# LSH attention and gated MLP on one core: one GpSimd addition for two heads, dearer planned residual loads, wide zero products, first low words on GpSimd

## The chip, the cores and the metric

One Trainium2 chip, one of its cores. The metric is the time of one execution on the device in microseconds (us); the median of several executions is compared. Engines: PE is TensorE, DVE is VectorE, ACT is ScalarE, POOL is GpSimd, SP is SyncE, which issues nearly all the DMAs here.

## The reference, cut to what matters

Batch 4, 8 heads, 768 positions, head size 64; then a gated MLP of width 512 with 1024 hidden columns.

```python
q_bits = (einsum(q, proj) > 0); k_bits = (einsum(k, proj) > 0)      # 6 bits, a bucket each
scores = where(q_bucket == k_bucket, q @ k.T / 8, -1e9)
attn = exp(scores - max); attn = attn / (sum(attn) + 1e-9)
x = concat_heads(attn @ v)
h = gelu(x @ w_in); u, v = split(h)
v_s = w_sg @ (layer_norm(v) * g_ln) + b_sg
out = x + (u * v_s) @ w_out
```

## The kernel before, in words

Every tensor that goes through PE in one pass is split into a high part (rounded by ACT) and a low part (the rest), and products are made of high and low parts. Work is done on pairs of heads: 16 pairs, the 128 partitions holding two heads of 64.

**For each pair** `load` brings q and k (the raw tile of each has one buffer, so the next pair's load waits until the last reader of the raw tile is done), `parts` transposes them on PE (line 543, six products each), copies them back by ACT (553), and makes the high part on ACT (547) and the low part on DVE (550). The first pair's bit features come from two products per tensor with `pwd` (586) and comparisons on DVE (589); the later pairs' features (570, 573) are scattered by DMA. `largest` makes the scores of one tile of 128 queries and takes the row maxima on DVE (616, 621); it runs `AHEAD` = 4 tiles ahead. `weigh` makes transposed scores of a key tile (656), the exponentials for both heads on ACT (661), and adds them up over the key tiles on POOL (674): before, one addition of 384 columns for each head, 5 additions per head and half, 320 in all, 64 of which are the first of a sum and read two tiles p. `weighted` makes p times v (686) and `total` the sums over partitions (710); `finish` sends sums through DRAM, takes reciprocals (729) and writes x transposed to DRAM (735).

**Between the pairs** twelve weight jobs (395 to 405: seven operations on DVE, one on POOL and one on ACT each) decode the MLP weights. **The MLP** follows batch by batch: `load_x` (835 to 840), `hidden_v` (882), `hidden_u` (913), `gate` (931), `project` (960). In the first batch, `gate_weights` also loads the transposed gate weights (851), transposes them on DVE (852), and splits them on ACT (853) and POOL (854), tile by tile, in a ring with eight buffers, so that a later tile's load waits until an earlier tile's transposition has begun. `project` adds the residual: `rx` is loaded from DRAM with 512 runs of 128 bytes per DMA (953), four DMAs for each tile of 128 positions, and transposed by DVE (956). It has two buffers.

**The order.** No engine's order is written by hand. Every operation is given to `Plan.add` with an engine, a planned cost, and a priority (smaller goes first). `Plan.order` simulates the engines with these costs and takes for each engine the ready operation with the smallest priority; the resulting order is then fixed in the program. In the real run every engine and every DMA queue goes through its list in that order and waits at the head of it. A planned cost is thus no time on the chip; it decides what stands behind what. Operations marked `port` (the POOL ones, and DVE ones with two SBUF operands) are planned so that POOL and DVE exclude each other. The numbers at the top of the file are offsets to priorities: `HID` to `hidden_v` of the first batch, `MLP` to its weights and loads, `SHAPE` and the `O.` lists to single operations.

**The lead** (lines 453 to 458) has zero products on PE before the first q arrives: five and four products of 128 columns of zeros, with six small transpositions between them in the source, which in the trace run after all nine.

```python
nc.tensor.matmul(psb[:, 6, :P], msts[0][:, 0].bitcast(F32), msts[0][:, 0].bitcast(F32), start=True, stop=True)   # 453, 458
dma(p0 - 30, 0.4, lambda eng, rx=rx, g=g, t=t: eng.dma_start(...), xd[b], [(rx, g)])                             # 953
```

Of the kernel before, what the change touches and what calls it, by code (L numbers as in the profile page):

```python
# [9 lines left out]
F32 = mybir.dt.float32  # L10
# [8 lines left out]
DRAM = bass.MemoryType.DRAM  # L19


MLP = {"xl": "POOL", "gm": "DVE", "gl": "POOL", "wg": 457.72, "wo": -69.99, "x": 480}

NSUM = 3
BANKED = False
HID = 267.73
AVP = 3.07
S0P = -1.32
AHEAD = 4
PREP, SHIFTP, FINP, WSTEP, WP = 10.27, -7.36, 10, 9.69, 23.41  # L30
LOADS = "SP"
GPLACE = 4
XLATE = 5.18
FIRST = -5
FEAT = 3.92
LOWP = 8.16
LOADP = 1.16
LATF = 3.2
OM = [0.01, 0.27, 0.0, 2.44, 0.37, 0.0, -1.25, 0.68, 0.49, 1.13, -0.06, 0.0]
OW = [0.0, 0.2, 0.0, 0.29, 0.0, 0.0, 0.0, 0.0, -0.69, 0.48, 0.0, 1.07]  # L40
# [3 lines left out]
OL = [-0.28, -0.4]  # L44
OH = [2.49, 0.0]
OT = [1.05, 0.73]
OF = [1.53, -2.21]
RATE = 2.73
WFROM = 1.42
ADDW = 1  # L50


SHAPE = {"A": [-0.81, -2.62, -0.81, -0.81, -0.81, -0.12, -0.81, -2.53, -0.81, -0.81, -0.81, -0.81, -0.81, -0.81, -0.81, -0.81, -0.81, -3.5, -0.81, -0.81], "AV": [0.04, 0.0], "C": [4.55, 2.17, 2.17, 4.28], "E": [0.0, 0.0, -1.65, -0.24, 1.16, 0.0, 0.0, 0.0, 0.36, 0.0, -2.01, 0.0], "M": [0.0, 0.0, 0.0, 0.0, 0.0, 0.0, 0.0, 0.0, 0.0, -0.91, 0.0, 0.0], "R": [0.0, 0.0, 0.0, 0.0, 0.0, 0.0, 0.0, -0.16, 0.0, -1.68, 0.0, 0.0], "S": [3.78, 0.75], "T": [0.0, 0.1], "W": [0.0, 0.0, 0.0, 0.0, 0.0, 0.0, 0.0, 0.0, 0.0, 0.0, 0.0, 0.0], "hi": [3.88, -3.27], "lo": [0.0, 0.0], "m": [1.89, -3.45], "rc": [-2.26, 0.77], "sm": [3.72, -0.88], "un": [1.1, 4.96], "xt": [3.13, -0.6], "F": [-0.28], "sg": [-0.66], "x": [0.35, 0.35]}


class Plan:
# [218 lines left out]
def kernel(  # L275
# [16 lines left out]
    nc = tc.nc  # L292

    B, H, S, D = q.shape
    P = 128
    NT = S // P
    HT = NT // 2
    SH = S // 2
# [10 lines left out]
    Q = 32  # L309
# [22 lines left out]
    msts = [const.tile([P, HT, P], F32R, name=f"m{i}") for i in range(2)]  # L332
# [78 lines left out]
    PE, DVE, ACT, POOL, SP = "PE", "DVE", "ACT", "POOL", "SP"  # L411
    xs = [dram.tile([DM, S], F32, name=f"xs_{b}") for b in range(B)]

    plan = Plan()
# [5 lines left out]
    xd = [[plan.buf(f"xd_{b}_{c}", 1) for c in range(NC)] for b in range(B)]  # L420
# [28 lines left out]

    ps_s = Pool("ps_s", "left", PSUM)  # L450
    psb = ps_s.pool.tile([P, 8, 512], F32, name="psb", tag="psb", bufs=1)
    for i in range(5):
        nc.tensor.matmul(psb[:, 6, :P], msts[0][:, 0].bitcast(F32), msts[0][:, 0].bitcast(F32), start=True, stop=True)
    for i in range(6):
        nc.tensor.transpose(psb[:, 7, i:i + 1], frow[:, i, :], ident[:1, :1])
    nc.vector.tensor_copy(fcol, psb[:, 7, 0:6])
    for i in range(4):
        nc.tensor.matmul(psb[:, 6, :P], msts[0][:, 0].bitcast(F32), msts[0][:, 0].bitcast(F32), start=True, stop=True)
    for s in range(2):
        for j in range(2):  # L460
            for r in range(2):
# [12 lines left out]
    if True:  # L474
# [61 lines left out]
        def parts(st, s, prio):  # L536

            hh, lo, raw, fac, tp = st.hi[s], st.lo[s], st.raw[s], (SCALE, 1.0)[s], ps_two()

            def tr():  # L540
                for hf in range(2):
                    for i in range(HT):
                        nc.tensor.transpose(tp()[:, hf, i * P:(i + 1) * P],
                                            raw()[:, hf * HT + i].rearrange("p j d -> p (j d)"), ident)

            def high():
                nc.scalar.mul(hh(), x_of(raw), fac)

            def low():
                nc.vector.scalar_tensor_tensor(lo(), x_of(raw), fac, hh().bitcast(F32), op0=ALU.mult, op1=ALU.subtract)  # L550

            plan.add(PE, 0.654, prio, tr, [raw], [tp], tag="T")
            plan.add(ACT, 0.81, prio, lambda: nc.scalar.copy(x_of(raw).rearrange("p (a b) -> p a b", a=2), tp()[:, :, :SH]), [tp], [raw], tag="x")
            def split(p1, p2):
                plan.add(ACT, 0.81, p1 + OH[s], high, [raw], [hh], tag="hi")
                plan.add(DVE, 0.98, p2 + OL[s], low, [raw, hh], [lo], port=True, tag="lo")

            st.split.append(split)

        def x_of(raw):  # L560
            return raw().rearrange("p t j d -> p (t j d)")
# [193 lines left out]
        def rest(st, prio):  # L755
# [32 lines left out]
        for n in range(NPAIR):  # L788
            for c in range(NT):
                if c == 0 and n + 2 < NPAIR:  # L790
                    prepare(n + 2, 2 * (g_ := NT * n) + PREP)
                hf, k0, g = c // HT, 2 * (c % HT), NT * n + c
# [9 lines left out]
                if c == 1 and GPLACE <= n < GPLACE + NT:  # L802
                    t = n - GPLACE
# [11 lines left out]

    M_ = MLP
    b1, b2 = Pool("b1", "right"), Pool("b2", "right")
# [5 lines left out]

    g_bc = b2.ring([P, FH], F32, "g_bc")

    def dma(prio, us, fn, r=(), w=(), e=SP):
        eng = nc.sync if e == SP else nc.scalar
        plan.add(e, 0.55, prio, lambda: fn(eng), r, w, dma=us)

    def load_x(b, prio):  # L830
        r = []
# [115 lines left out]
    def project(b, gs, prio):  # L947
        ov = out[b].rearrange("(t p) m -> p t m", t=NT)
        for t in range(NT):
            ts_, hf, p0 = slice(t * P, (t + 1) * P), t // HT, prio + t  # L950
            rx, po, ob = tile_of([P, DM], F32, "rx", 2), ps_one(), tile_of([P, DM], F32, "ob", 2)
            for g in range(P // Q):
                dma(p0 - 30, 0.4, lambda eng, rx=rx, g=g, t=t: eng.dma_start(
                    rx()[g * Q:(g + 1) * Q].rearrange("b (f a) -> b f a", a=Q),
                    xs[b][:, t * P + g * Q:t * P + (g + 1) * Q].rearrange("(f b) a -> b f a", b=Q)), xd[b], [(rx, g)])
            plan.add(DVE, 0.7, p0 - 5, lambda rx=rx, ob=ob: nc.vector.transpose(ob(), rx()), [rx], [ob])
            for f, (gh, gl) in enumerate(gs):
                def mm(f=f, gh=gh, gl=gl, po=po, ts_=ts_):
                    for n, (a, w) in enumerate(((gh, woh), (gh, wol), (gl, woh))):
                        nc.tensor.matmul(po(), a()[:, ts_], w()[:, f, :], start=(f == 0 and n == 0), stop=(f == NF - 1 and n == 2))  # L960
                plan.add(PE, 0.685, p0 + 0.01 * f, mm, [(gh, hf), (gl, hf), (woh, f), (wol, f)], [po])

            plan.add(DVE, 0.7, p0, lambda ob=ob, po=po: nc.vector.tensor_add(ob(), po(), ob()), [po, ob], [ob])  # L963
            dma(p0, 0.73, lambda eng, ob=ob, t=t: eng.dma_start(ov[:, t, :], ob()), [ob])


    xx = load_x(0, HID - 20)
# [55 lines left out]
```

## Time and profile before

| | |
|---|---|
| median of three executions | 734.95 us (734.49 to 736.82) |
| the profiled execution | 734.26 us, of it 732.5 us from the first to the last instruction |
| PE busy | 719.4 us, 98% of the span |
| DVE, POOL, ACT busy | 529.2, 471.7, 381.0 us |
| mean granted clock of PE | 0.998 |

The busy times are shares of the whole span; the stages differ, and PE's busy time includes the modelled end of each product. The table of stages among the rows below shows where PE is not busy. A row of the timeline gives the start, how long a run of equal instructions lasts, the engine, the line, and in brackets the idle time before it with what ended it.

### The profile page before, as it was taken

The numbers are of one execution on the slowest core, as the hardware profiler recorded it, in microseconds if no ns is written. First come the engines' busy times: TensorE is split into PE (matmuls) and PEld (weight loads), VectorE is DVE, ScalarE is ACT, GpSimd is POOL, SyncE is SP. The second block draws the span as 40 slices with busy tenths as digits, with TensorE's granted clock in tenths as the row PEclk, the third lists the DMA queues.
The fourth block names the chain that finished last, engine by engine and source line by source line (L and its number), as shares of the span: only waits on it lengthen the run. The fifth ranks groups of instructions, "written<-read, shape, count | busy, mean of one in ns | idle before, by whom it ended". The sixth has DMA issues, their size and how long they took to land. (4 is left out here: it accounts for less than half of the span.)

```text
span 732.5 us, 14275 instructions
## 1 busy us (share of the span) xinstructions
PE 719.4 (98%) x5304; PEld 570.6 (78%) x5304; DVE 529.2 (72%) x783; ACT 381.0 (52%) x611; POOL 471.7 (64%) x452
## 2 busy tenths in 40 slices
PE   8999999999999999999999999999999999999997
PEld 6777676766767676776767669888999889988996
DVE  6888779997899998788899258455863586348733
ACT  2666576666657656665756547421761066106510
POOL 2589799998898987897898957551553045404230
PEclk9999999999999999999999999999999999999999
DMA  6314643644665455255532135814221601061004
GB/s 129 85 44 103 132 130 94 136 106 124 166 143 133 103 117 139 68 133 137 136 101 65 59 110 138 193 48 127 47 65 37 146 14 44 0 148 26 0 1 116
DMA packets 177766, 70.39 MB, mean 96 GB/s; under 512 B 157728, under 2 KB 167968, under 8 KB 177696
## 3 DMA queue, kind: packets, MB, share of 16 engines
q1 hardware_dynamic: 176464, 68.62, 39.1%
q8 instruction: 42, 0.69, 0.5%
q10 hardware_dynamic: 1232, 0.86, 0.4%
q14 instruction: 28, 0.23, 0.1%
HBM read 51.61 MB, written 17.24 MB: 94 GB/s over the span
## 5 line engine op out<-in xcount | busy, mean ns | idle before, releaser
L674 POOL TENSOR_TENSOR sum<-sum,p 128x384 f32<-128x384 f32 x256 | 247.1, 991 | 44.5 <-ACT p L661 39.5
L621 DVE TENSOR_REDUCE mx<-psb 128x2 f32<-128x768 f32 x192 | 175.7, 951 | 38.0 <-PE psb L616 36.8
L661 ACT ACTIVATE p<-psb 128x768 f32<-128x768 f32 x192 | 149.8, 815 | 25.8 <-PE psb L656 17.3
L686 PE MATMUL psb<-p,v 128*64 128x385 f32 x768 | 131.2, 491 | 0.0
L686 PEld LDWEIGHTS psb<-p,v 128*64 128x64 f32 x768 | 52.3, 137 | 71.7 <-issue 62.7
L674 POOL TENSOR_TENSOR sum<-p,p 128x384 f32<-128x384 f32 x64 | 82.2, 1304 | 18.4 <-ACT p L661 18.4
L656 PE MATMUL psb<-hq,hk 64*128 64x384 f32 x384 | 71.6, 368 | 0.9 <-DVE mx L621 0.6
L616 PE MATMUL psb<-fk,fq 64*128 64x384 f32 x384 | 67.3, 345 | 2.9 <-DVE mx L621 2.6
L892 POOL TENSOR_TENSOR mv<-mv,epsr 128x1 f32<-128x1 f32 x24 | 14.0, 583 | 86.3 <-DVE mv L891 67.3
L942 POOL TENSOR_TENSOR gs<-gt,gs 128x384 fp32r<-128x384 f32 x32 | 33.3, 1046 | 53.1 <-ACT gs L939 47.2
L931 PE MATMUL psb<-wgl,zh 128*128 128x384 f32 x192 | 64.4, 335 | 1.2 <-POOL wgl L854 1.2
L931 PE MATMUL psb<-wgh,zh 128*128 128x384 f32 x192 | 64.4, 335 | 1.1 <-DVE u L871 1.1
L616 PE MATMUL psb<-hk,hq 64*128 64x384 f32 x384 | 65.1, 333 | 0.0
L656 PE MATMUL psb<-lq,hk 64*128 64x384 f32 x384 | 64.8, 333 | 0.0
L656 PE MATMUL psb<-fq,fk 64*128 64x384 f32 x384 | 64.8, 333 | 0.0
L656 PE MATMUL psb<-hq,lk 64*128 64x384 f32 x384 | 64.7, 332 | 0.0
L931 PE MATMUL psb<-wgh,zl 128*128 128x384 f32 x192 | 64.2, 334 | 0.0
L866 ACT ACTIVATE h<-psb 128x384 f32<-128x384 f32 (+1 forms) x56 | 29.4, 534 | 64.8 <-PE psb L882 54.2
L960 PE MATMUL psb<-woh,gs 128*128 128x512 f32 x192 | 59.8, 389 | 0.0
L701 ACT COPY un<-psb 128x385 f32<-128x385 f32 x32 | 15.4, 480 | 84.3 <-PE psb L686 84.3
L934 DVE TENSOR_TENSOR gt<-psb,b_bc 128x384 f32<-128x384 f32 x32 | 17.8, 556 | 44.5 <-PE psb L931 41.8
L939 ACT CAST gs<-gt 128x384 fp32r<-128x384 f32 x32 | 16.4, 514 | 61.9 <-DVE gt L938 61.9
(120 smaller groups left out, 1576.3 us busy)
## 6 DMA issues: line engine op xcount, KB each, us to landing
q<-in_q_dram SPq DMA_DIRECT2D x32, 192.0 KB
v<-in_v_dram SPq DMA_DIRECT2D x16, 384.0 KB
rs<-r SPq DMA_DIRECT2D x64, 96.0 KB
xs<-xt SPq DMA_DIRECT2D x32, 192.0 KB
x<-xs SPq DMA_DIRECT2D x16, 384.0 KB
rx<-xs SPq DMA_DIRECT2D x96, 64.0 KB
out_dram<-ob SPq DMA_DIRECT2D x24, 256.0 KB
k<-in_k_dram SPq DMA_DIRECT2D x31, 192.0 KB
```

Source lines behind the costliest of these rows:

```text
L616: nc.tensor.matmul(sc[kh]()[:, j, :SH], x[0]()[row(j), qs], x[1]()[row(j), kh * SH:(kh + 1) * SH], start=(n == 0), stop=(n == 1))
L621: plan.add(DVE, 0.95, prio + OM[2 * t + kh], lambda kh=kh: nc.vector.tensor_reduce(mx()[:, i, :, kh], sc[kh]()[:, :, :SH], axis=AX.X, op=A ...
L656: nc.tensor.matmul(sc[i]()[:, j, :SH], x()[row(j), ks], y()[row(j), cs], start=(n == 0), stop=(n == 3))
L661: plan.add(ACT, 0.81, prio, lambda i=i: nc.scalar.activation(p[i]()[:, :, :SH], sc[i]()[:, :, :SH], AF.Exp), [sc[i]], [p[i], ticks[-1]], t ...
L674: plan.add(POOL, 1.03, prio + 0.6, lambda i=i, j=j, first=first: nc.gpsimd.tensor_add(sums()[:, j], (first or sums)()[:, j, :SH], p[i]()[: ...
L686: nc.tensor.matmul(av()[row(j), :SH + 1], v_()[:, j, kt, :], p[kt]()[:, j, :], start=(kt == 0), stop=(kt == NT - 1))
L866: plan.add(ACT, ua - 0.02, prio, lambda: nc.scalar.activation(h2()[:, :n], ps()[:, :n], AF.Square), [ps], [h2])
L931: nc.tensor.matmul(vp()[:, :SH], z()[:, t, fs], w()[:, t, cs], start=(t == 0 and n == 0), stop=(t == NT - 1 and n == 2))
L934: plan.add(DVE, 0.56, p0, lambda vp=vp, gt=gt, cs=cs: nc.vector.tensor_add(gt(), vp()[:, :SH], b_bc()[:, cs]), [vp, b_bc], [gt])
L939: plan.add(ACT, 0.51, p0, lambda gt=gt, gh=gh, cs=cs: nc.scalar.copy(gh()[:, cs], gt()), [gt], [(gh, hf)])
L942: nc.gpsimd if e == POOL else nc.vector).tensor_sub(gl()[:, cs], gt(), gh()[:, cs].bitcast(F32)),
L960: nc.tensor.matmul(po(), a()[:, ts_], w()[:, f, :], start=(f == 0 and n == 0), stop=(f == NF - 1 and n == 2))
```

## The change

Four edits and a new set of priorities. `ADDW = 2` picks the branch that adds the exponentials of both heads in one POOL operation of 2 x 384 columns, planned at 1.88 us where the two single ones were planned at 1.03 each. The residual loads' planned SP time goes from 0.55 to 0.8 us, their planned transfer from 0.4 to 0.7, and their priority offset from 30 to 9.55. The zero products become three of 384 columns and one of 128. For the first pair (`st.n` = 0) the copy by ACT also multiplies by the scale, the high part is taken with factor 1, and the low part is a subtraction on POOL and no longer on DVE. The constants at the top are new, cut here to those that the prediction names; `SHAPE` and the other offsets change by up to some units each.

```diff
-MLP = {"xl": "POOL", "gm": "DVE", "gl": "POOL", "wg": 457.72, "wo": -69.99, "x": 480}
+MLP = {"xl": "POOL", "gm": "DVE", "gl": "POOL", "wg": 456.91, "wo": -41.91, "x": 458.24}
...
-HID = 267.73
+HID = 304.61
...
+RXP = 9.55
...
-RATE = 2.73
-WFROM = 1.42
-ADDW = 1
+RATE = 2.72
+WFROM = 1.22
+ADDW = 2
...
-    for i in range(5):
-        nc.tensor.matmul(psb[:, 6, :P], msts[0][:, 0].bitcast(F32), msts[0][:, 0].bitcast(F32), start=True, stop=True)
+    zeros = msts[0].rearrange("p a b -> p (a b)").bitcast(F32)
+    for i in range(3):
+        nc.tensor.matmul(psb[:, 6, :SH], msts[0][:, 0].bitcast(F32), zeros, start=True, stop=True)
...
-    for i in range(4):
-        nc.tensor.matmul(psb[:, 6, :P], msts[0][:, 0].bitcast(F32), msts[0][:, 0].bitcast(F32), start=True, stop=True)
+    nc.tensor.matmul(psb[:, 6, :P], msts[0][:, 0].bitcast(F32), msts[0][:, 0].bitcast(F32), start=True, stop=True)
...
+            scale, fac = (fac, 1.0) if not st.n else (1.0, fac)
...
-            plan.add(ACT, 0.81, prio, lambda: nc.scalar.copy(x_of(raw).rearrange("p (a b) -> p a b", a=2), tp()[:, :, :SH]), [tp], [raw], tag="x")
+            plan.add(ACT, 0.81, prio, lambda: nc.scalar.mul(x_of(raw).rearrange("p (a b) -> p a b", a=2), tp()[:, :, :SH], scale), [tp], [raw], tag="x")
...
+                if not st.n:
+                    plan.add(POOL, 1.88, p2 + OL[s], lambda: nc.gpsimd.tensor_sub(lo(), x_of(raw), hh().bitcast(F32)), [raw, hh], [lo])
+                    return
...
-                dma(p0 - 30, 0.4, lambda eng, rx=rx, g=g, t=t: eng.dma_start(
+                dma(p0 - RXP, 0.7, cost=0.8, fn=lambda eng, rx=rx, g=g, t=t: eng.dma_start(
```

The branch that `ADDW = 2` picks stands in the kernel before, in `weigh`:

```python
plan.add(POOL, 1.88, prio + 0.6, lambda i=i, first=first: nc.gpsimd.tensor_add(
    sums(), (first or sums)()[:, :, :SH], p[i]()[:, :, :SH]), [p[i]] + ([first] if first else []), [sums])
```

## Rows read from the trace of the kernel before

**Rows 1.** Busy time by stage: start:end length, PE, PEld, DVE, ACT, POOL, granted clock, DMA

```profile
0.00:24.00 24.00, 20.47 (x111) 15.75 (x113) 16.65 (x51) 8.61 (x11) 3.69 (x18) 0.93 0.50 99
24.00:426.00 402.00, 398.60 (x3660) 281.11 (x3658) 331.93 (x402) 252.16 (x388) 353.16 (x335) 1.00 0.47 112
...
458.00:492.00 34.00, 31.61 (x171) 29.68 (x171) 15.51 (x28) 11.63 (x21) 18.24 (x13) 1.00 0.53 128
492.00:729.00 237.00, 236.76 (x1204) 216.03 (x1202) 138.74 (x254) 86.97 (x154) 77.44 (x71) 1.00 0.25 58
```

**Rows 2.** Timeline of PE in the lead, 0 to 14 us

```profile
1.32 2.50 PE L453 MATMUL psb<-m 128*128 128x128 f32 x10 [1.32 <-DVE m L333]
3.61 1.91 PE L458 MATMUL psb<-m 128*128 128x128 f32 x8
...
6.18 1.54 PE L543 MATMUL psb<-ident,q 128*128 128x128 f32 x6
...
8.79 2.26 PE L586 MATMUL psb<-q,pwd 128*128 128x384 f32 x4
10.89 1.45 PE L586 MATMUL psb<-k,pwd 128*128 128x384 f32 x4
12.51 0.44 PE L616 MATMUL psb<-fk,fq 64*128 64x384 f32 x2 [0.17 <-DVE fk L589]
```

**Rows 3.** Timeline of PE at 171 us, the same transposition later

```profile
171.12 0.88 PE L543 MATMUL psb<-ident,k 128*128 128x128 f32 x6
```

**Rows 4.** Busy time in single microseconds (columns as in rows 1)

```profile
18.00:19.00 1.00, 1.00 (x7) 1.00 (x6) 1.00 (x2) 0.00 (x0) 0.00 (x0) 0.50 0.00 0
```

**Rows 5.** Timeline of ACT in the lead

```profile
7.76 0.80 ACT L553 COPY q<-psb 128x768 f32<-128x768 f32 x1 [1.22 <-PE psb L543]
8.59 0.84 ACT L547 ACTIVATE hq<-q 128x768 fp32r<-128x768 f32 x1
9.34 0.78 ACT L553 COPY k<-psb 128x768 f32<-128x768 f32 x1
```

**Rows 6.** Timeline of DVE in the lead

```profile
12.98 0.95 DVE L550 SCALAR_TENSOR_TENSOR lk<-k,hk 128x768 fp32r<-128x768 f32 x1
13.85 5.27 DVE L621 TENSOR_REDUCE mx<-psb 128x2 f32<-128x768 f32 x6
```

**Rows 7.** Timeline of POOL in the lead, its first addition

```profile
26.25 1.99 POOL L674 TENSOR_TENSOR sum<-p,p 128x384 f32<-128x384 f32 x2 [18.20 <-ACT p L661]
```

**Rows 8.** Line 674: durations in ns, shortest, median, longest; first and last start

```profile
L674 POOL TENSOR_TENSOR sum<-sum,p x256: 853/1000/1722, 28.2 to 426.3; 128x384 f32<-128x384 f32 x128
L674 POOL TENSOR_TENSOR sum<-p,p x64: 995/1398/1775, 26.3 to 418.4; 128x384 f32<-128x384 f32 x64
```

**Rows 9.** Line 838, POOL operations of 768 columns

```profile
L838 POOL TENSOR_TENSOR xl<-x,xh x16: 1834/1858/2538, 103.2 to 622.5; 128x768 fp32r<-128x768 f32 x16
```

**Rows 10.** Waits for POOL's sums: engine, line, releaser: us in total, times, longest

```profile
PEld psb L710 <- POOL sum L674: 0.8, 3, 0.2
```

**Rows 11.** Groups of instructions, line 550: busy us, mean ns, idle before

```profile
L550 DVE SCALAR_TENSOR_TENSOR lq<-q,hq 128x768 fp32r<-128x768 f32 x16 | 24.3, 1518 | 1.2 <-ACT hq L547 1.2
L550 DVE SCALAR_TENSOR_TENSOR lk<-k,hk 128x768 fp32r<-128x768 f32 x16 | 21.4, 1340 | 0.0
```

**Rows 12.** Busy time in 80 us of the attention (columns as in rows 1)

```profile
186.00:266.00 80.00, 79.83 (x744) 56.39 (x742) 73.05 (x88) 51.37 (x79) 70.39 (x68) 1.00 0.59 137
```

**Rows 13.** Timeline of SP's queue, 455 to 466 us

```profile
455.19 10.34 SPq L953 DMA_DIRECT2D rx<-xs  x8
465.57 0.49 SPq L851 DMA_DIRECT2D gs<-wgd  x1
```

**Rows 14.** Timeline of DVE at 466 us

```profile
465.97 0.71 DVE L956 STREAM_TRANSPOSE ob<-rx 128x512 f32<-128x512 f32 x1 [4.33 <-DMA rx<-xs]
```

**Rows 15.** Timeline of PE, 470 to 482 us

```profile
470.70 0.44 PE L931 MATMUL psb<-wgh,zh 128*128 128x384 f32 x1 [1.15 <-DVE u L871]
...
481.04 0.45 PE L931 MATMUL psb<-wgl,zh 128*128 128x384 f32 x1 [1.21 <-POOL wgl L854]
```

More of the change, by code (lines that the diff above doesn't have):

```diff
@@ L29 @@
 AHEAD = 4
-PREP, SHIFTP, FINP, WSTEP, WP = 10.27, -7.36, 10, 9.69, 23.41
+PREP, SHIFTP, FINP, WSTEP, WP = 10.15, -4.79, 9.31, 9.56, 22.97
 LOADS = "SP"
 GPLACE = 4
-XLATE = 5.18
+XLATE = 5.15
 FIRST = -5
-FEAT = 3.92
-LOWP = 8.16
-LOADP = 1.16
+RXP = 9.55
+FEAT = 2.68
+LOWP = 7.25
+LOADP = 2.29
 LATF = 3.2
@@ L47 @@
 OF = [1.53, -2.21]
-RATE = 2.73
-WFROM = 1.42
-ADDW = 1
-SHAPE = {"A": [-0.81, -2.62, -0.81, -0.81, -0.81, -0.12, -0.81, -2.53, -0.81, -0.81, -0.81, -0.81, -0.81, -0.81, -0.81, -0.81, -0.81, -3.5, -0.81, -0.81], "AV": [0.04, 0.0], "C": [4.55, 2.17, 2.17, 4.28], "E": [0.0, 0.0, -1.65, -0.24, 1.16, 0.0, 0.0, 0.0, 0.36, 0.0, -2.01, 0.0], "M": [0.0, 0.0, 0.0, 0.0, 0.0, 0.0, 0.0, 0.0, 0.0, -0.91, 0.0, 0.0], "R": [0.0, 0.0, 0.0, 0.0, 0.0, 0.0, 0.0, -0.16, 0.0, -1.68, 0.0, 0.0], "S": [3.78, 0.75], "T": [0.0, 0.1], "W": [0.0, 0.0, 0.0, 0.0, 0.0, 0.0, 0.0, 0.0, 0.0, 0.0, 0.0, 0.0], "hi": [3.88, -3.27], "lo": [0.0, 0.0], "m": [1.89, -3.45], "rc": [-2.26, 0.77], "sm": [3.72, -0.88], "un": [1.1, 4.96], "xt": [3.13, -0.6], "F": [-0.28], "sg": [-0.66], "x": [0.35, 0.35]}
+RATE = 2.72
+WFROM = 1.22
+ADDW = 2
+SHAPE = {"A": [0.62, -1.19, 0.62, -0.38, 0.62, 1.31, 0.62, -1.1, 0.62, 0.62, 0.62, 0.62, -0.96, 0.62, 0.62, 0.62, 0.62, -2.07, 0.62, 0.62], "AV": [0.04, 0.0], "C": [3.79, 2.41, 3.53, 3.52], "E": [0.0, 0.0, -1.65, -0.24, 1.16, 0.0, -0.63, 2.51, 0.36, 0.0, -2.01, 0.0], "M": [0.0, 0.0, 0.0, 0.0, 0.0, -0.21, 0.0, 0.0, 0.0, -0.91, 0.0, -1.94], "R": [0.6, 0.6, 1.13, 0.6, -0.6, 0.6, 0.6, 0.44, 0.6, -1.08, 0.6, 0.6], "S": [0.18, 1.75], "T": [0.47, 0.68], "W": [0.0, 0.0, 0.0, 0.0, 0.0, 0.0, 0.0, 0.0, 0.0, 0.0, 0.0, 0.0], "hi": [3.88, -3.27], "lo": [0.0, -1.87], "m": [1.19, -3.45], "rc": [-3.68, 1.0], "sm": [4.69, -0.03], "un": [2.6, 6.46], "xt": [7.81, 0.51], "F": [-1.53], "sg": [-3.33], "x": [0.35, 1.9]}
 class Plan:
@@ L824, with dma @@
     g_bc = b2.ring([P, FH], F32, "g_bc")
-    def dma(prio, us, fn, r=(), w=(), e=SP):
+    def dma(prio, us, fn, r=(), w=(), e=SP, cost=0.55):
         eng = nc.sync if e == SP else nc.scalar
-        plan.add(e, 0.55, prio, lambda: fn(eng), r, w, dma=us)
+        plan.add(e, cost, prio, lambda: fn(eng), r, w, dma=us)
     def load_x(b, prio):
@@ L952, in project @@
             for g in range(P // Q):
-                dma(p0 - 30, 0.4, lambda eng, rx=rx, g=g, t=t: eng.dma_start(
+                dma(p0 - RXP, 0.7, cost=0.8, fn=lambda eng, rx=rx, g=g, t=t: eng.dma_start(
                     rx()[g * Q:(g + 1) * Q].rearrange("b (f a) -> b f a", a=Q),
-                    xs[b][:, t * P + g * Q:t * P + (g + 1) * Q].rearrange("(f b) a -> b f a", b=Q)), xd[b], [(rx, g)])
+                    xs[b][:, t * P + g * Q:t * P + (g + 1) * Q].rearrange("(f b) a -> b f a", b=Q)), r=xd[b], w=[(rx, g)])
             plan.add(DVE, 0.7, p0 - 5, lambda rx=rx, ob=ob: nc.vector.transpose(ob(), rx()), [rx], [ob])
```

## The prediction, before the changed kernel was run

> **What bounds the kernel now.** I read the table of stages first. PE is busy 398.60 of 402 us in the attention, 236.76 of 237 in the later batches, and leaves time open in three places: 3.53 us before 24 us, 3.40 spread over the attention, 2.39 between 458 and 492 us [rows 1]. After 729 us only the last addition and its store remain, which the change does not touch. So no edit can gain much more than these 9.3 us plus what PE does slowly, and an edit on another engine counts only where PE waits for it. The second view is the timeline of the lead. The same product with 384 columns takes 2.26 us for q and 1.45 us for k right behind it, and six transpositions take 1.54 us at 6.18 where they take 0.88 later [rows 2, 3]. The column of the granted clock does not show this early stretch, so I go by the durations: their ratio is near that of 2.4 to 1.2 GHz, and the clock rose during q's products, at about 10 us. It falls once more: 0.50 at 18 us, after the stretch in which DVE's maxima set the pace [rows 4, 6]. The third view is SP's queue in the transition: eight residual loads hold it for 10.34 us, 1.29 each, against a planned 0.55 [rows 13].
>
> **Sum of probabilities in one operation.** It removes 320 POOL operations and adds 160. A 768-column POOL operation takes 1.86 us at the median [rows 9]. Two of the 256 single ones take 2.00 at their medians and 1.71 at their shortest, so 128 merged ones cost between 19 us less (at 1.86 against 2.00, 18) and 19 more (1.86 against 1.71). Two first additions take 2.80 at the median, 1.99 at best [rows 8]; 32 merged ones then cost 30 us less or 4 less. I take 18 + 4 = 22 us less POOL time. On the path this is worth nothing: PE waits 0.8 us in all for sums [rows 10], the first and last sum of a half come as early as before, and the saved time only lengthens POOL's idle stretches, which are 49 us of 402 [rows 1]. Bounds: 0.8 gained, and a loss that is the first rival below.
>
> **First low words on POOL.** POOL has nothing between its memsets and the first addition, an idle of 18.20 us [rows 7], so two subtractions of 1.86 us are covered and nothing queues behind them. Their first reader is the weighing, whose exponentials reach POOL at 26.25. The raw tiles are released when these subtractions end: q's high part ends at 9.43, its low part near 11.3, k's near 13.2 where DVE's ended at 13.93, so the next pair's loads are no later [rows 5, 6]. DVE loses the 0.95 us at 12.98 that stood between the features and the first maximum at 13.85 [rows 6]. The first maximum needs PE's products from 12.51, four of some 0.4 us with overlap, done near 13.3: **0.5 us** gained, bounds 0 and 0.95. The scaled copy by ACT costs 0.84 instead of 0.80 [rows 5]: nothing beside that.
>
> **Wide zero products.** Before, nine products run from 1.32 to 5.52, 0.47 each. A 384-column product at the low clock takes between 1.13 (half of q's 2.26, whose end is fast already) and 1.45 us (twice half of k's 1.45); with 1.28, three and one narrow one take 4.31, **0.1 us more** if the clock stays low [rows 2]. No row shows the clock after wide zero products; the nearest are the wide products with q, the last thing before the clock rose, while nine narrow ones and twelve transpositions ran without a rise. If the wide zeros bring it up before q's transposition, this is 0.66 shorter, so ACT's copy starts 0.66 - 0.1 = 0.56 earlier; ACT's chain copy, high, copy ends at 9.56 instead of 10.12, q's products start at 8.23 and take 1.45, and k's start at 9.7 instead of 10.89 [rows 2, 3, 5]. That is 1.2 us. If the zeros themselves ran fast, they would give up to half of their 3.84 us on top, 3.1 in all, unless q's arrival, which no row dates, stops it. Between 0.1 lost and 3.1 gained I take **1.2**, which needs the fast clock from q on only. The Trainium skill, TensorE: Matmul & The Clock Gate, Part 1, says that the release depends on how long PE has been kept busy and not on which or how many products; by it narrow zeros serve as well and the wide ones bring nothing. This trace speaks against it, with a clock still low after nine busy microseconds.
>
> The low clock at 18 us slows the second pair's transpositions by about 0.66 each. The shift may move them in or out of it: 1.3 either way, taken as 0.
>
> **Residual loads planned longer, and the MLP's numbers.** In the plan an operation outranks another by priority alone. `HID` moves first-batch hidden work from 267 to 304, still above every attention priority (about 215 at most) and below 430, so it reorders nothing. `wo` (430 to 458) and the 30 to 9.55 (670 to 690 for the first batch) pass no other DMA on SP either: the gate loads stand at 952, stores at 700 and above. `x` comes down from 980 to 958 and now competes with the gate weights' split (957 to 962) on ACT and POOL: a subtraction of 1.86 us could stand ahead of one that PE waits for. What does act is the cost: the plan now sees eight loads take 6.4 us instead of 4.4, where the chip takes 10.34. DVE stood 4.33 us at the transposition of the first residual tile, and behind it waited the hidden work that frees PE's banks: PE's 1.15 us at 470.70 [rows 13 to 15]. Planned later by 2 us, that wait shrinks but stays: I take **0.8** of the 1.15. The 1.21 at 481.04 comes from the last gate tile, whose load still stands behind the residual loads; it stays. Bounds: all 2.39 gained, 1.86 lost.
>
> **New priorities in the attention.** PE's 3.40 us of idle are a dozen stalls of 0.1 to 1.5 us; another order has others. Zero, bounds 3.4 gained, and the rival below lost.
>
> **Sum:** 0.5 + 1.2 + 0.8 = 2.5 us, so 731.8 for an execution like the profiled one at 734.26. The median lies 0.69 above it, so I forecast 732.4, 0.35% below 734.95. A measurement can tell about 0.3%, 2.2 us, from no change.
>
> **Rival 1, slower: DVE waits for the longer additions.** DVE's operations with two SBUF operands stretch where POOL is active: 0.95 alone at 12.98, 1.52 and 1.34 on average for the 32 low words, 0.48 us of waiting each [rows 6, 11]. The code has some 148 such operations in the attention (32 low words, 32 of line 735, 84 in weight jobs), about 29 in 80 us. The Trainium skill, SBUF — State Buffer, "two separate sides", says that the pair of ports is locked for a whole instruction, so the loser waits to its end. If the wait doubles with the addition's length, 29 x 0.48 = 14 us come on in the fullest 80 us, where DVE has 6.95 idle [rows 12]; 7 us then fall on PE, which waits for maxima: 739.6. Against it: POOL starts half as many operations, and the plan knows the longer occupation. It decides from about 0.24 us more per operation, and outweighs the gains and the 0.3% from 0.40.
>
> **Rival 2, same: the clock stays low in the lead.** The 1.2 becomes a loss of 0.1: 732.4 + 1.3 = 733.7. For it: nine zero products and the transpositions behind them did not raise it before.
>
> **Rival 3, faster still: the attention's stalls go.** With POOL less occupied and the order new, PE's 3.40 us vanish: 729.0. Against it: only 0.8 us of waiting was POOL's.
>
> **How the numbers follow.** The forecast's mechanism has 0.47, rival 1 0.18, rival 2 0.23, rival 3 0.12. The forecast lies 0.35 us below the 0.3% line (732.75), so I put 0.36 of its 0.47 below that line and 0.11 above it; rival 3 adds 0.12: faster 0.48. Same: 0.11 + 0.23 = 0.34. Slower 0.18. The range reaches from 728.0 (rival 3 and a further us of the transition) to 737.5, which takes in rival 2 and the milder half of rival 1; about 0.1 is left out above and 0.07 below.
>
> **What would show it.** Right: q's transposition near 0.9 us, k's feature products from about 9.7, the first maximum near 12.2, POOL's first addition near 24.5, no low word on DVE before 20 us; line 674 160 times near 1.9 us; PE's idle in the attention still near 3.4; a shorter stall of PE near 470. Wrong: q's transposition still at 1.5 us (rival 2); low words over 1.9 us on average and PE idle for line 621 beyond 8 us (rival 1); a merged addition near 2.5 us, which would fill POOL.

## The result and the profile after

The changed kernel takes 727.17 us (median, 726.39 to 727.57), the kernel before 734.72 in the same runs: 0.99 of it, interval 0.9877 to 0.9923, or 7.6 us less. In two later sessions it took 726.45 and 726.32 us. The forecast was 732.4 and the range began at 728.0: the sign was right, the size was three times as large. The profiled execution has a span of 725.8 us against 732.5.

Busy time by stage of the changed kernel (columns as in rows 1):

```profile
0.00:22.00 22.00, 19.03 (x109) 11.36 (x109) 16.25 (x50) 8.93 (x12) 7.29 (x20) 1.00 0.57 108
22.00:424.00 402.00, 399.93 (x3668) 281.40 (x3664) 332.22 (x401) 251.76 (x390) 311.30 (x176) 1.00 0.48 113
...
456.00:490.00 34.00, 34.00 (x183) 32.17 (x182) 16.61 (x29) 10.62 (x20) 17.51 (x13) 1.00 0.39 98
```

PE's open time fell from 3.40 to 2.07 us in the attention and from 2.39 us to nothing in the transition [rows 1]. The second holds in every later profile of this order; the first doesn't: the same kernel was profiled twice more (e11, e14), and its attention has 2.35 and, here in e14 (columns as in rows 1), 3.69 us open:

```profile
22.00:424.00 402.00, 398.31 (x3654) 280.70 (x3651) 329.18 (x400) 251.22 (x388) 310.91 (x176) 1.00 0.47 112
```

To split the whole span I took four marks on PE: the first product of the weighing that reads a low word, the last product p times v, the first output product, the last output product. Before they stand at 23.87, 426.15, 487.22 and 728.38 us, after at 20.66, 421.65, 479.37 and 720.52. The first of them, before and after:

```profile
23.87 0.34 PE L656 MATMUL psb<-hq,lk 64*128 64x384 f32 x2
...
20.66 0.33 PE L662 MATMUL psb<-hq,lk 64*128 64x384 f32 x2
```

So the **lead** gives 3.2 us, the **attention** 1.3, the stretch from there **to the first output product** 3.35, all of it in the gate stage (from the first product of `gate` to the first output product, 28.34 against 24.97 us); between the output marks both take 241.2, and the tail takes 1.2 more (5.27 against 4.10). With the same instructions on PE, later executions had tails of 4.1 to 4.2, so that the last 1.2 is not the change's. The lead and the gate stage repeat in e11 and e14 (20.45 and 20.24; 24.96 both). The attention's 1.3 is not firm: the changed kernel takes 400.99, 401.32 and 402.53 us there, the order of before 402.28 and 403.06 (e1).

The gate stage gains more than its 2.39 us of open time, since that counts from the modelled end of a product. Of the 144 products of that stage, the changed kernel starts one every 0.17 us throughout. The kernel before has 1.48 us from this one to the one at 470.70 [rows 15]:

```profile
469.22 0.34 PE L931 MATMUL psb<-wgh,zl 128*128 128x384 f32 x1
```

With the 1.54 us at the second stall and five slower starts this makes 3.3 us.

The lead, PE of the changed kernel:

```profile
1.32 4.21 PE L455 MATMUL psb<-m 128*128 128x384 f32 x6 [1.32 <-DVE m L334]
...
6.26 0.88 PE L544 MATMUL psb<-ident,q 128*128 128x128 f32 x6
...
9.61 1.56 PE L592 MATMUL psb<-k,pwd 128*128 128x384 f32 x4
11.29 0.44 PE L622 MATMUL psb<-fk,fq 64*128 64x384 f32 x2
...
16.49 0.87 PE L544 MATMUL psb<-ident,q 128*128 128x128 f32 x6 [0.26 <-DVE mx L627]
17.36 0.44 PE L622 MATMUL psb<-fk,fq 64*128 64x384 f32 x2
...
18.56 0.84 PE L544 MATMUL psb<-ident,k 128*128 128x128 f32 x6
```

DVE in the lead:

```profile
8.99 1.32 DVE L595 TENSOR_SCALAR fq<-psb,fcol 128x384 fp32r<-128x384 f32 x2 [2.44 <-PE psb L592]
10.56 1.32 DVE L595 TENSOR_SCALAR fk<-psb,fcol 128x384 fp32r<-128x384 f32 x2 [0.25 <-PE psb L592]
12.02 5.28 DVE L627 TENSOR_REDUCE mx<-psb 128x2 f32<-128x768 f32 x6
```

POOL in the lead:

```profile
8.94 1.82 POOL L560 TENSOR_TENSOR lq<-q,hq 128x768 fp32r<-128x768 f32 x1 [1.46 <-ACT hq L550]
10.72 1.82 POOL L560 TENSOR_TENSOR lk<-k,hk 128x768 fp32r<-128x768 f32 x1
23.98 1.84 POOL L676 TENSOR_TENSOR sum<-p,p 128x768 f32<-128x768 f32 x1 [11.43 <-ACT p L667]
```

And one microsecond at which the kernel before had its clock at 0.50 [rows 4]:

```profile
18.00:19.00 1.00, 0.68 (x7) 0.68 (x8) 1.00 (x2) 0.97 (x2) 0.00 (x0) 1.00 0.00 0
```

q's first transposition takes 0.88 us, not 1.54; the first maximum starts at 12.02, not 13.85, with no low word ahead of it; and there is no second fall of the clock: the second pair's transpositions, back to back and slow before, take 0.87 and 0.84 with score products between them.

The groups of the additions, before, and of the merged additions and DVE's low words, after:

```profile
L674 POOL TENSOR_TENSOR sum<-sum,p 128x384 f32<-128x384 f32 x256 | 247.1, 991 | 44.5 <-ACT p L661 39.5
L674 POOL TENSOR_TENSOR sum<-p,p 128x384 f32<-128x384 f32 x64 | 82.2, 1304 | 18.4 <-ACT p L661 18.4
...
L676 POOL TENSOR_TENSOR sum<-sum,p 128x768 f32<-128x768 f32 x128 | 225.6, 1762 | 82.2 <-ACT p L667 74.5
L676 POOL TENSOR_TENSOR sum<-p,p 128x768 f32<-128x768 f32 x32 | 61.2, 1914 | 11.7 <-ACT p L667 11.6
...
L553 DVE SCALAR_TENSOR_TENSOR lk<-k,hk 128x768 fp32r<-128x768 f32 x15 | 25.1, 1674 | 0.0
L553 DVE SCALAR_TENSOR_TENSOR lq<-q,hq 128x768 fp32r<-128x768 f32 x15 | 20.4, 1362 | 0.3 <-issue 0.3
```

The additions take 287 us of POOL where they took 329 (247.1 + 82.2), 42 less. k's low words did get longer, 1674 ns against 1340, and q's shorter, 1362 against 1518 [rows 11].

SP's queue in the transition:

```profile
444.30 1.02 SPq L857 DMA_DIRECT2D gs<-wgd  x1
...
449.53 7.99 SPq L959 DMA_DIRECT2D rx<-xs  x8
457.56 0.49 SPq L857 DMA_DIRECT2D gs<-wgd  x1
```

And DVE at the first residual tile:

```profile
458.55 0.71 DVE L962 STREAM_TRANSPOSE ob<-rx 128x512 f32<-128x512 f32 x1 [1.18 <-DMA rx<-xs]
```

Before, the last gate tile:

```profile
473.66 0.49 SPq L851 DMA_DIRECT2D gs<-wgd  x1
```

Now it is asked for at 457.56 us, where before the last but one was at 465.57; the first eight residual loads end at 457.5 and not at 465.5, and DVE's stall at them is 1.18 us instead of 4.33 [rows 13, 14].

### The profile page after: what moved, and what is told of

The parts are those of the page before. It is cut to its first block, busy times and chain, and to the rows that moved or that the text cites. A ratio compares the mean times of both kernels' runs of the same rounds, so it can differ in the third digit from the quotient of the medians.

```text
span 725.8 us, 14083 instructions
## 1 busy us (share of the span) xinstructions
PE 715.9 (99%) x5294; PEld 565.4 (78%) x5294; DVE 528.9 (73%) x781; ACT 380.2 (52%) x611; POOL 430.9 (59%) x294
## 4 chain that ended last, share of the span: by engine, by line
PE 93%; DVE 3%; SPq 1%; DMA 1%; ACT 1%; issue 1%; DVEq 0%; ACTq 0%
PE psb L662 18%; PE psb L692 16%; PE psb L937 14%; PE psb L888 9%; PE psb L919 9%; PE psb L966 9%; PE psb L622 8%; PE psb L544 3%; DVE mx L627 2%; PE psb L716 2%; PE psb L576 1%; PE psb L640 1%; PE psb L455 1%; SPq L812 1%; DMA w<-in_moe_w_in_dram 0%
## 5 line engine op out<-in xcount | busy, mean ns | idle before, releaser
L676 POOL TENSOR_TENSOR sum<-sum,p 128x768 f32<-128x768 f32 x128 | 225.6, 1762 | 82.2 <-ACT p L667 74.5
L676 POOL TENSOR_TENSOR sum<-p,p 128x768 f32<-128x768 f32 x32 | 61.2, 1914 | 11.7 <-ACT p L667 11.6
L873 DVE SCALAR_TENSOR_TENSOR h<-h,psb 128x384 f32<-128x384 f32 (+1 forms) x56 | 32.9, 603 | 28.4 <-ACT h L872 28.3
```

The source lines that it names most:

```text
L676: plan.add(POOL, 1.88, prio + 0.6, lambda i=i, first=first: nc.gpsimd.tensor_add(sums(), (first or sums)()[:, :, :SH], p[i]()[:, :, :SH]), ...
L873: plan.add(DVE, us + 0.07, prio, lambda: nc.vector.scalar_tensor_tensor(h2()[:, :n], h2()[:, :n], 1.0 / GA, ps()[:, :n], op0=ALU.add, op1= ...
```

## The experiments

Eighteen runs were made in five sessions. The kernel before had medians of 733.63 us (e1 to e4), 733.27 (e5 to e8), 734.04 (e9 to e12), 734.29 (e13 to e16) and 735.41 (e17, e18); a difference below is against the median of its own session. "Order" is what the planner makes of costs and priorities.

### The low words

**e8**, the kernel before with the low-word edit alone:

```diff
+            scale, fac = (fac, 1.0) if not st.n else (1.0, fac)
...
+                if not st.n:
+                    plan.add(POOL, 1.88, p2 + OL[s], lambda: nc.gpsimd.tensor_sub(lo(), x_of(raw), hh().bitcast(F32)), [raw, hh], [lo])
...
```

> The kernel before with the first pair's low words on GpSimd alone. The planner then puts products of line 616 between the two transpositions of the second pair. Theory A2: the first maximum follows the first product of line 616 by 0.75 instead of 1.34 us, and the low clock at 17 us is gone: 0.5 plus 1.3, so 1.3 to 2.2 us faster than before, 731.4 to 732.5. Rival: the clock falls again, 0.5 us faster at most.

729.40 us, ratio 0.9948 (0.9929 to 0.9967): **3.9 us**, where I had 0.5, and beyond both expectations. PE of e8 in the lead:

```profile
15.97 0.88 PE L543 MATMUL psb<-ident,q 128*128 128x128 f32 x6 [0.25 <-DVE mx L626]
16.84 0.44 PE L621 MATMUL psb<-fk,fq 64*128 64x384 f32 x2
...
18.04 0.84 PE L543 MATMUL psb<-ident,k 128*128 128x128 f32 x6
...
19.80 0.34 PE L661 MATMUL psb<-hq,lk 64*128 64x384 f32 x2
```

The planner, which has DVE freer, puts score products between the second pair's two transpositions, and the clock does not fall here. The mark of the first low-word product comes at 19.80 us, 4.1 earlier; the gate stage is 1.8 us shorter and the attention 2.2 longer. Not all of the 4.1 is the order's: the clock rose at 5.0 us here and at 10.4 in the profile of before. e10 below has the lead of before, a rise at 4.3 us and no fall:

```profile
21.30 0.34 PE L656 MATMUL psb<-hq,lk 64*128 64x384 f32 x2
```

Against this mark the order is worth 1.5 us; the other 2.6 go with the clock. And e8 has a low clock elsewhere, in its attention, right behind PE's longest wait (a row of the timeline, then busy time, columns as in rows 1):

```profile
168.58 0.50 PE L621 MATMUL psb<-fk,fq 64*128 64x384 f32 x2 [2.25 <-DVE mx L626]
...
169.00:172.00 3.00, 3.00 (x20) 2.56 (x17) 2.96 (x5) 1.21 (x2) 3.00 (x4) 0.50 0.30 112
```

So a part of the 2.2 us is the clock's too.

**e5**, the changed kernel's order with the two subtractions on DVE all the same:

```diff
-                    plan.add(POOL, 1.88, p2 + OL[s], lambda: nc.gpsimd.tensor_sub(lo(), ...
+                    plan.add(POOL, 1.88, p2 + OL[s], lambda: nc.vector.tensor_sub(lo(), ...
```

> The changed kernel in its own order, the first pair's two low words subtracted by VectorE at the same place of the order instead of by GpSimd. Theory A2 (the low words give the lead's gain): the first maximum comes 0.5 to 1.0 us later after the first product of line 616, and the stretch of maxima ends later; 0.5 to 1.0 us slower than the changed kernel, 727.2 to 728.2, and over 1.5 slower if the low clock at 17 us comes back. Rival (VectorE's time there is covered by PE): within 0.3 us.

726.43 us, 0.9911 (0.9889 to 0.9932). Its lead, from q's transposition to the first low-word product:

```profile
5.62 0.88 PE L544 MATMUL psb<-ident,q 128*128 128x128 f32 x6
...
20.93 0.34 PE L662 MATMUL psb<-hq,lk 64*128 64x384 f32 x2
```

That is 15.31 us against 14.40, so the place of the two operations is worth 0.9 in the lead, about the upper bound of my term; the whole time shows none of it. By exclusion, what e8 gains is then the order that the edit leads to, with the clock under it; no profile splits its 3.9 us further.

### The merged additions

**e4**, the kernel before with one number turned:

```diff
-ADDW = 1
+ADDW = 2
```

> The kernel before with merged additions alone (same numbers otherwise; the planner orders anew). Here all six gate-tile loads stand ahead of the residual loads in SP's queue, where before had four. Theory B (the merged additions make the transition's gain): PE's idle between 458 and 492 us falls from 2.4 to under 0.5, the lead stays: 2.5 to 4.5 us faster, 730.2 to 732.2. Theory C (the prediction's: the dearer planned residual loads make it): the transition still has more than 1.5 us of idle and the time is within 1.5 us of before, 733.2 to 736.2.

731.58 us, 0.9965 (0.9948 to 0.9982): **2.1 us**, where I had 0. Its lead is that of before, late rise and fall included. Attention 400.50 us (402.28 before, 403.06 in e1); SP's residual loads start at 452.80 and take 6.74 us, and PE's stalls in the gate stage are 0.66, 0.55 and 0.27 us, 1.48 in all: the time is theory B's, the stalls did not go as far as it said.

**e3**, the changed kernel with the same entry of the plan (1.88 us), issued as two single additions:

```diff
-                    plan.add(POOL, 1.88, prio + 0.6, lambda i=i, first=first: nc.gpsimd.tensor_add(
-                        sums(), (first or sums)()[:, :, :SH], p[i]()[:, :, :SH]), [p[i]] + ([first] if first else []), [sums])
+                    plan.add(POOL, 1.88, prio + 0.6, lambda i=i, first=first: [nc.gpsimd.tensor_add(
+                        sums()[:, j], (first or sums)()[:, j, :SH], p[i]()[:, j, :SH]) for j in range(2)], [p[i]] + ([first] if first else []), [sums])
```

> The changed kernel in its own order on every engine, but each merged addition is issued as two single ones of 384 columns, as before. Theory B1 (the merged operation itself is what helps, since POOL is late at the attention's end): POOL's busy time in the attention goes from 311 back to about 345 us, the last sums come several us after the last exponential and the time rises by 2 to 4 us, 729 to 731. Theory B2 (what helps is the order that the planner makes with 1.88 instead of 2 x 1.03): the order is kept, so it stays within 1 us, 726.5 to 728.2.

726.71 us, 0.9895 (0.9878 to 0.9912), no slower than the changed kernel. Its additions by duration:

```profile
L676 POOL TENSOR_TENSOR sum<-sum,p x256: 849/998/1739, 27.3 to 421.5; 128x384 f32<-128x384 f32 x128
```

256 single operations, as before [rows 8], and all of the gain. So the merged operation itself is worth nothing that shows, as forecast; e4's 2.1 us come from the order planned with it.

**e7**, the changed kernel without it:

```diff
-ADDW = 2
+ADDW = 1
```

> The changed kernel with the additions single and planned so (2 x 1.03); the planner orders anew, four gate tiles stand ahead of the residual loads as in the kernel before. Theory B (the merged plan gives the transition and part of the attention): the transition has 2 to 3 us of PE idle again and the attention takes 1 to 2 us more: 3 to 5 us slower than the changed kernel, 730 to 732. Rival (the new priorities do it): within 1.5 us, 726 to 728.7.

735.96 us, 1.0042 (1.0018 to 1.0065): all of the gain is lost, more than either expectation allowed. PE's waits of e7 in the attention (22 to 424 us; us in total, times, longest):

```profile
PE psb L622 <- ACT p L667: 4.2, 2, 2.2
PE psb L662 <- DVE mx L627: 0.8, 2, 0.4
```

The score products stand behind exponentials, a wait that the changed kernel doesn't have, and the attention takes 406.12 us. Behind the wait of 2.2 us, which ends at 140.85, the clock is low here too (columns as in rows 1):

```profile
142.00:145.00 3.00, 3.00 (x24) 2.99 (x20) 2.43 (x4) 0.86 (x2) 2.92 (x4) 0.50 0.01 0
```

**e16**, the kernel before with all the new numbers but that one:

```diff
-HID = 267.73
+HID = 304.61
...
-RATE = 2.73
-WFROM = 1.42
+RATE = 2.72
+WFROM = 1.22
 ADDW = 1
```

> The kernel before with the planner's new numbers alone (single additions, low words on VectorE, narrow zeros). Theory that the new numbers bring nothing without the merged additions: 733 to 737 us, attention 402 to 407 us. Rival, that the new numbers shorten the attention by themselves: 731 us or less, attention 401 us or less.

736.67 us, 1.0033 (1.0015 to 1.005), attention 405.11, with the same kind of wait (2.82 us, to 141.13) and a clock of 0.50 from 143 to 145: the numbers fit the merged plan and harm the single one. Over the profiles, orders planned with single additions have attentions of 402.3 to 406.1 us (before, e1, e7, e8, e10, e16; in e7, e8 and e16 with a low clock inside), those planned with merged ones 399.5 to 402.7 (all the others). The ranges touch, and the changed kernel alone spreads over 1.5 us.

### Both, and what is left for the plan of the transition

**e15**, the kernel before with e8's edit and e4's, nothing else:

```diff
-ADDW = 1
+ADDW = 2
...
+            scale, fac = (fac, 1.0) if not st.n else (1.0, fac)
```

> The kernel before with two of the four edits alone: first low words by GpSimd and merged additions (narrow zero products, old plan of the residual transfers, old numbers of the planner). Theory that these two carry nearly all of the gain, by the order that the planner makes of them (3.9 and 2.1 us each alone): 726.5 to 728.5 us, first weighing product at 20 to 22 us, attention 400 to 402 us, gate stage up to the first output product 24.9 to 26 us. Rival, that wide zeros, the dearer residual plan or the new numbers are needed for the last part: 729.5 to 731 us.

728.32 us, 0.9921 (0.9897 to 0.9945): 5.97 us, the sum of the two alone (3.87 + 2.05). It stands inside the bounds given, but its gate stage did not come out as expected: 27.8 us and not 24.9 to 26. PE there:

```profile
456.34 0.45 PE L936 MATMUL psb<-wgh,zl 128*128 128x384 f32 x1 [0.86 <-POOL zl L903]
458.20 0.45 PE L936 MATMUL psb<-wgh,zh 128*128 128x384 f32 x1 [1.42 <-DVE u L876]
```

2.3 us of stalls, and the changed kernel on the same chip (e14) was 2.0 us faster. Not all of the 2.0 need be the stalls: the mean granted clock was 0.998 in three of e15's five executions and 0.999 or more in e14's four. What removes the stalls: **e6**, the changed kernel with the residual loads planned as before,

```diff
-                dma(p0 - RXP, 0.7, cost=0.8, fn=lambda eng, ...
+                dma(p0 - 30, 0.4, cost=0.55, fn=lambda eng, ...
```

> The changed kernel with the residual loads planned as before (0.55, 0.4, offset 30); the planner orders the MLP anew, five gate tiles still stand ahead of the residual loads. Theory C (the prediction's: the dearer plan takes VectorE's wait for the first residual tile off PE): PE's idle between 455 and 490 us comes back by 0.8 us or more, 727.8 to 729. Theory B (the gate tiles' place does it): no idle there, within 0.5 us of the changed kernel, 726.5 to 727.7; the stores at the end again stand between the residual loads.

727.32 us, 0.9923 (0.9901 to 0.9944), gate stage 25.1 us; and **e9**, the four edits with the numbers of before:

```diff
-HID = 304.61
+HID = 267.73
...
 ADDW = 2
```

> The four edits with the numbers of the kernel before at the top of the file (ADDW = 2, RXP = 9.55). Here all six gate tiles stand ahead of the residual loads. If the edits alone make the gain (low words 3.9 us in one run, merged additions 2.1 in another): 5 to 7.5 us faster than before, 726 to 728.5. Rival (the new priorities are needed): 3 us or less gained, over 730.

727.23 us, 0.9912 (0.9895 to 0.9928), gate stage 25.9 us, one stall of 0.7 us. So the dearer loads do it without the new numbers, and the new numbers without the dearer loads; only where both are missing (e15) is the stall back. Either takes 1.9 to 2.7 us off e15's gate stage, the second one 0.2 to 0.9. The wide zeros, which e15 lacks as well, have no part in it: with narrow ones (e2, e13, e17) the gate stage takes 24.96 us.

**e10**, the kernel before with the gate weights ahead of the residual loads in priority, 600 for 958:

```diff
-MLP = {..., "wg": 457.72, ...}
+MLP = {..., "wg": 100, ...}
```

> The kernel before with the priority of the gate weights at 600 instead of 958 for the first batch, so that the fifth and sixth tile's loads stand ahead of residual loads in SP's queue, and their splits ahead of others. Theory B (the stalls at 470 and 481 us come from the gate tiles' place): PE's idle between 458 and 492 us falls from 2.4 to under 1 us, 1.4 to 2.4 us faster than before. Rival (the residual loads' own time and VectorE's wait for them make it): 1.1 us of idle or more stays, within 1.2 us of before.

732.85 us, 0.9984 (0.9966 to 1.0002), the rival's bounds, with 1.93 us of PE's stalls left. SP's queue of e10:

```profile
454.48 1.09 SPq L851 DMA_DIRECT2D gs<-wgd  x1
455.62 9.42 SPq L953 DMA_DIRECT2D rx<-xs  x8
...
465.62 0.43 SPq L851 DMA_DIRECT2D gs<-wgd  x1
```

One more gate tile passes the residual loads, and PE's stall at 470 is gone. DVE waits 0.96 us for the first residual tile, though 3.41 for that gate tile. The last one still stands behind eight loads, and PE waits for it as before:

```profile
476.31 0.44 PE L931 MATMUL psb<-wgl,zh 128*128 128x384 f32 x1 [1.63 <-POOL wgl L854]
```

So a priority alone did not move it. From the code I take it that the ring of buffers holds it back; that was not tried.

### The zero products and the clock

**e1**, the kernel before with the wide zeros alone:

```diff
+    zeros = msts[0].rearrange("p a b -> p (a b)").bitcast(F32)
+    for i in range(3):
+        nc.tensor.matmul(psb[:, 6, :SH], msts[0][:, 0].bitcast(F32), zeros, start=True, stop=True)
...
```

> The kernel before with the wide zero products alone; the order of everything else is that of before. Theory A (the clock is up from q's transposition on): the first product of line 616 comes at about 11.5 us instead of 12.51, and the low clock at 17 to 20 us goes or stays by chance: 1.0 to 2.5 us faster than before, some 732.2 to 733.7. Rival (the wide products bring nothing by themselves): q's transposition still takes 1.5 us and the time is within 0.5 us of before.

733.91 us, 1.0008 (0.9996 to 1.0019): nothing. **e2**, the changed kernel with the nine narrow zeros:

```diff
-    for i in range(3):
-        nc.tensor.matmul(psb[:, 6, :SH], msts[0][:, 0].bitcast(F32), zeros, start=True, stop=True)
+    for i in range(5):
+        nc.tensor.matmul(psb[:, 6, :P], msts[0][:, 0].bitcast(F32), msts[0][:, 0].bitcast(F32), start=True, stop=True)
...
```

> The changed kernel with the nine narrow zero products of before in the lead, all other orders as changed. Theory A: the clock rises at about 10 us again, the first maximum comes 1.2 us later (13.2 instead of 12.0) and the second pair's transpositions may fall under the low clock again: 1.2 to 2.6 us slower than the changed kernel, 728.4 to 729.8. Rival (the lead's gain comes from the moved low words): within 0.5 us of the changed kernel.

728.25 us, 0.9922 (0.9907 to 0.9937), between the two expectations, with a rise at 10.7 us and no fall. **e12**, the changed kernel with none (beside **e11**, the changed kernel):

```diff
-    for i in range(3):
+    for i in range(0):
...
-    nc.tensor.matmul(psb[:, 6, :P], msts[0][:, 0].bitcast(F32), msts[0][:, 0].bitcast(F32), start=True, stop=True)
```

> The changed kernel without any zero product in the lead (they reach no result); all orders otherwise as changed. If zero products do anything for the clock, it rises at 9 us or later in this run, q's transposition takes 1.5 us and the time is 1 to 2 us over the changed kernel. If they do nothing, the same time within 0.7 us.

> The changed kernel once more, beside the others on one chip, and a second profile of it: 726 to 728. If the early rise of the clock belongs to the wide products it rises before 6 us again; if it is a matter of chance it may rise at 10 to 11 us, with the first weighing 1.0 to 1.5 us later than at 20.66.

727.60 us, 0.9919 (0.9901 to 0.9936), and 726.45, 0.9898 (0.9881 to 0.9915); without zeros the rise came at 11.5 us. **e13**, narrow zeros again, beside **e14**, the changed kernel:

> The changed kernel with nine zero products of 128 columns in place of six of 384, on one chip with the changed kernel itself (the next run). Theory that the width of the zero products is worth nothing and that the early or late rise of the granted clock (4.3 to 6.1 us against 10.2 to 10.7 us so far) is a matter of the execution: both medians within 1 us of each other, and the clock rises at about the same time in both profiles. Rival, that wide products bring the rise forward: this one rises at 10 to 11 us where the next rises at 4 to 6 us, and is slower by 1.0 to 1.6 us.

> The changed kernel, on one chip with the run ahead of it: 726 to 728 us by both theories. Theory of no effect: its median within 1 us of the run ahead. Rival: it is 1.0 to 1.6 us faster and its clock rises at 4 to 6 us while the other's rises at 10 to 11 us.

727.48 us, 0.9909 (0.9883 to 0.9935), and 726.32, 0.9897 (0.987 to 0.9924): the rival's marks, a late rise (10.0 us) and 1.16 us. Then **e17** and **e18**, e13's and e3's programs once more:

> The same kernel as the run with narrow zeros beside the changed one, which had its clock rise at 10.0 us and a median of 727.48 us. Theory that the program with narrow zeros always rises late: rise at 10 to 11 us, 727 to 728.5 us. Rival, that the rise is a matter of the execution: it may rise at 4 to 6 us here (a rise there settles it for the rival; a late rise leaves it open).

> The changed kernel's order with its merged additions issued as two single ones, again: it has the wide zeros and the changed kernel's instructions on PE, and its profile showed a rise at 10.4 us where the changed kernel showed 4.6 to 5.7 us. Theory that the rise is a matter of the execution: it may rise at 4 to 6 us here, with a median of 725 to 727.5 us all the same. Rival, that something in this program holds the clock back: a rise at 10 to 11 us again.

727.03 us, 0.9888 (0.9864 to 0.9912), and 725.68, 0.9867 (0.9843 to 0.9891). q's first transposition in e13, narrow zeros:

```profile
6.18 1.54 PE L544 MATMUL psb<-ident,q 128*128 128x128 f32 x6
```

in e17, the same program:

```profile
6.09 0.87 PE L544 MATMUL psb<-ident,q 128*128 128x128 f32 x6
```

in e3, wide zeros:

```profile
6.61 1.54 PE L544 MATMUL psb<-ident,q 128*128 128x128 f32 x6
```

in e18, the same program as e3:

```profile
6.52 0.87 PE L544 MATMUL psb<-ident,q 128*128 128x128 f32 x6
```

One program shows both, so the program alone doesn't set the moment of the rise. A late one costs 1.1 us at the mark of the first low-word product (21.64 against 20.50, 22.05 against 20.92). In all profiles the record of the clock rises at 4.3 to 6.4 us or at 10.0 to 10.7; early in eight of ten with wide zeros (not in e1, e3), in five of nine with narrow ones (e8, e10, e15, e16, e17), and at 11.5 us with none (e12). By session it was late in all of e1 to e4 and early in all of e5 to e11, and each of the two pairs of one program ran on two chips, so that chip and execution are not told apart.

Still, in the changed order the wide zeros were ahead in each session: 726.71 against 728.25 (e3, e2), 726.45 against 727.60 for none, 726.32 against 727.48, 725.68 against 727.03, thus by 1.2 to 1.5 us, though the intervals of each pair overlap. Execution by execution the gap is plainer in one pair: all five of e3 (724.89 to 727.21) lie below all six of e2 (727.37 to 728.63). But e3 and e18 have single additions besides; e13 and e14 differ in the zeros alone, and their executions overlap. More early rises among the unprofiled executions would explain it. No run here shows that, and the profiles of e2 and e3 speak against it: both rise late and have the mark at 22.05, and the 2.3 us between their spans are 1.2 in the attention and 1.1 in the tail. In the order of before e1 has no gain. The size of this part stays open between 0 and 1.5 us.

## Why the prediction was wrong in size

**First low words on POOL, "0.5 us gained": the step that failed most, mis-sized by 3.4 us.** The edit alone gave 3.9 us (e8). The two operations are what I took them for: 1.82 us each, covered, and 0.9 us in the lead when they are put back (e5). But I costed a move on a list of operations, and what is fixed is an order made by a planner. With DVE free earlier the planner places score products between the second pair's transpositions, worth 1.5 us in the lead beside e10 with the clock up in both, and the orders behind it change up to the gate stage. That the rest is the order's too is argued by exclusion.

**Low clock at 18 us, "1.3 either way, taken as 0".** I had the price and no sign. The fall is in the three profiles with a late rise and DVE's low words ahead of the maxima (before, e1, e4), and in none of e2, e3 and e13, which rise as late with the new lead. There PE waited 1.0 us for the first maximum at 14.85, a wait that the new order lacks. e10 has it too (0.99 us), after an early rise, and no fall; so the wait alone isn't enough, and a late rise alone isn't either. Which of the waits lets the clock fall was not tried by itself. The sign shows over all executions beside these runs as well: the mean granted clock is 0.998 or less in 75 of the 80 of the kernel before, and 0.999 or more in all 12 of the changed kernel. So this term, held at 0, belongs on the gain's side; what it gives there, and where in an execution without a profile the clock is low, is not on record.

**Merged additions, "on the path this is worth nothing".** Right of the operation (e3), wrong of the edit: 2.1 us (e4). The cost in the plan falls from two times 1.03 to 1.88, and the order made with it has a shorter attention in e4's profile and asks for the residual and gate tiles earlier. POOL's saving was 42 us, not 22 (a merged running addition took 1.76 us on average and not 1.86, two single ones 1.98), and the path had none of it.

**Residual loads, "0.8 of the 1.15", and "the 1.21 ... stays".** Both stalls went: 2.39 us of open time, the bound I gave, and 3.35 from start to start, so that the bound itself was too low. The dearer plan is not what does it alone: without it the time is the same (e6). I said that nothing but the cost acted on SP's order; the order made from the whole set of edits brings the last gate tile from 473.66 to 457.56 us, and DVE's stall to 1.18. My step "it stays" failed, since I took SP's order to be the old one and judged the new priorities one by one.

**Wide zero products, "1.2".** The chain behind an early rise was right to the tenth: q's transposition 0.88, k's feature products at 9.61 against the 9.7 forecast. That wide products cause it is not shown; see above. The Trainium skill, TensorE: Matmul & The Clock Gate, Part 1, which I set against this trace, has it that the width doesn't matter; e17's early rise with narrow zeros agrees with it, and my argument from one late execution was too short. It also has the moment of the release vary by half a microsecond from run to run; one program here rose at 5.9 and at 10.0 us behind the same products.

**Rival 1** fell: k's low words did stretch by 0.33 us each, but q's shrank by 0.16, and PE waits 1.3 us in all for row maxima in the attention, not over 8; DVE is busy there for 332.22 us, against 331.93 before. Its time had a slip, too: 732.4 and 7 make 739.4, not 739.6. **Rival 2** is the late rise: real, 1.1 us, and not set by the program alone. **Rival 3** is not shown: 3.40 us of attention stalls before, and 2.07, 2.35 and 3.69 in three profiles of the changed kernel.

In sum: low words and merged additions 6.0 us together (e15), and 2.0 us from there to the changed kernel on the same chip (e14), by residual plan, numbers and zeros together; in the profiles that is the gate stage's stalls, while the attention differs the other way (399.48 us in e15, 402.53 in e14). The range began 0.8 us above the median since each edit's part in the planner's order was held at nothing.

## What to carry to other kernels

Where a planner makes the order, an edit of an operation or of a planned cost is an edit of the whole order: cost it by where the path's stalls are and by whether a new order could remove each, not by the edited instructions alone. To tell the two apart, keep the new order and put the old instruction back (e3, e5): here neither operation showed in the whole time, and the two edits together gave 6 us. Numbers tuned with one set of edits can be a loss without them (e16, e7), so that they are judged only together.

## What the runs showed of the hardware

The granted clock rose at 5.9 us in one execution and at 10.0 in another of one program, worth 1.1 us, so one profile can't tell what a warm-up brings. It fell to 0.50 (1.2 of 2.4 GHz) in three attentions, within 1.4 us of the end of a wait of PE of 2.20 (e7), 2.25 (e8) and 2.82 us (e16); waits of 2.00 us (e7), 2.02 (e16) and 2.21 us (e4) had no fall behind them, so that the length of the one wait doesn't decide. Eight residual loads held SP for 10.34 us before and for 7.99 here; e4 had 6.74 with the same eight loads, so an issue of 512 short runs took 0.84 to 1.29 us; what else was under way differed, and what decides was not tried. A running addition of 768 columns takes 1.69 us at the median on POOL, two of 384 take 2.00 [rows 8]:

```profile
L676 POOL TENSOR_TENSOR sum<-sum,p x128: 1673/1694/2295, 25.9 to 420.3; 128x768 f32<-128x768 f32 x128
```
